# One order list for the third to the eleventh tile of a fused spectral filter and gated MLP; late row blocks by three rounded products

## The chip, the cores and the metric

One Trainium2 chip, one core, one launch. The metric is device microseconds (us). All times come from the runs, or from one profiled execution of the program.

## The reference

```python
def _A_ref(x, w_r, w_i):
    X = jnp.fft.rfft2(x, axes=(-2, -1))
    X = X * (w_r + 1j * w_i)
    return jnp.fft.irfft2(X, s=(S, D), axes=(-2, -1))

def _B_ref(x, w_gate, w_up, w_down):
    g = jnp.einsum("bsd,df->bsf", x, w_gate)
    u = jnp.einsum("bsd,df->bsf", x, w_up)
    return jnp.einsum("bsf,fd->bsd", _gelu(g) * u, w_down)

h = x + _A_ref(_layernorm(x), A_w_r, A_w_i)
out = h + _B_ref(_layernorm(h), B_w_gate, B_w_up, B_w_down)
```

x is 1 x 2048 x 512 in float32, the filter 2048 x 257, the hidden width of the MLP 1376. The norms have no weights and an eps of 1e-5.

## The kernel before

The 2048 rows are 16 row blocks of 128; a row of a block stays on a partition. The tensor `gh` holds all of them, first x, then the filter's output, then the sum.

*The filter.* The transforms are products with constant matrices, in full float32. START orders the norm and the transform over rows, SECOND the transform over columns, the filter and the first half of the way back. What is left is, for each block, a product over columns with `dis` (`over_d_back`, name U), an unfolding of even and odd parts (names V, X, K) and a product over rows with `mis` (M for blocks 0 to 7, "late" for blocks 8 to 15), then the residual with x and the statistics of the second norm (`stats2`).

*The MLP.* The hidden width is 11 tiles of 128 (`NF`), the rows are two halves of 1024. A tile's gate and up products for half of the rows are seven sums P0 to P6 (a Winograd form: 7 products for 8), each of two pairs. A float32 number is split into a rounded high part in the type fp32r and a low part, so a pair is three rounded products (`mm3`, high x high, high x low, low x high). The left factors are `cb` (the normalized rows, `combine`), the right ones `gu` (`load_gu`): two DMAs into `raw`, four steps on POOL that form differences, then the high part in one cast on DVE (or on ScalarE, with `by=act`) and the low part in three steps on POOL, for P0, for P1 to P3 and for P4 to P6. `raw` is one buffer; `gu` is two. ScalarE copies c1, c2 and c3 and DVE sums d1, dy, d2 let TensorE go on in the same banks (P2 needs c1, P4 needs c2, P5 needs c3, P6 needs dy). G, m, i and o are the gelu, the product with the up side, the rounding and the low part. `load_d` loads and splits a tile's rows of the down matrix (`wdr`, `wd`; name w). The down products add groups of two or three tiles into `gh`, block by block, through the banks 6 and 7 (`down`).

Tiles 0 to 10 serve the first half of the rows, 11 to 21 the second half, whose norm is put in late.

*What sets the order.* START, SECOND and FIRST are lists of names: within `tc.manual_schedule` each named engine works in the list's order, and waits only for data. FIRST covers the rest of the filter for blocks 0 to 7, the tiles 0 and 1 in two halves of the rows, and the first product of tile 2 (`g2P0`). In it r0 to r3 are the four steps on the weights of tile 2, hc the cast, lo1 to lo3 the low parts.

Tiles 2 to 10 are not in a list. A loop over n calls a generator for each tile (`gate_up` through `step`), one for the down products (`down` through `fill`) and one for each late block (`late`); only TensorE is held to the loop's order, and the other engines are put in order by the scheduler, with hints (`tc.issue_after`, `held`, `behind`). A late block's steps are: unfold (four POOL instructions on 128x256), load x, one float32 product with `mis`, residual, statistics. The second half follows the table SECOND_HALF, in a manual schedule of its own.

SP issues nearly all DMAs, in its program's order; it is in no list.

Of the kernel before, what the change touches and what calls it, by code (L numbers as in the profile page):

```python
# [49 lines left out]
u0.1 u4.0 w4 C4.0 V4.2 X4 w0 C0.1 V0.3 X0 U1.2 C1.4 V1.0 X1 r0 U5.3 C5.5 V5.1 M4.1 O4.0 M0.2 O0.1 U2.3 H4 H0 X5 C2.5  # L50
V2.3 M5.1 H5 I4 G4 O5.0 G0 I0 S4 S0 A4 A0 E0.5 U7.2 C7.1 M1.3 O1.1 g0awh H1 Q0 N0 U6.0 C6.0 V7.4 X2 U3.4 C3.5 I5 G5 S5
M2.1 V6.3 R00 I1 G1 S1 A5 A1 R01 U9.7 C9 H2 X7 V3.1 X3 T00 a0 Q1 T01.2 s0.0 O2.1 U8.4 C8 E1.6 N1 R11 M7.0 c0 d0 f0
U12.3 e0.1 k0 R10 H7 b0 O7.0 g0 h0 C12 X6 M6.4 H6 i0 j0 T11.1 s1.2 r1 l0 T10 c1 d1 G2 I2 M3.2 O3.1 H3 G7 a1 b1 I7 S7
O6.0 U15.3 C15 e1.0 f1 g1 U14.5 C14 U10.4 C10 m0 k1 n1 g0aP0 g0ac1 g1aP0 l1 g0aP3 g0aP1 G3 I3 S3 A7 A3 Q3 g0aP2 I6 n0
G6 h1 g1ac1 E3.7 N3 g1aP2 i1 R31 T31.5 g1aP1 o1 R30 T30 S2 S6 A6 A2 g1ac2 j1 E2.6 Q2 N2 o0 g1aP4 g0awl s3.6 c3 g0ac2
g0aP4 R20 T20 a3 g1ac3 g1aP5 d3 e3.4 K9.5 m1 g0ad1 g0ac3 g0aP5 f3 b3 h3 g0ady g0aP6 i3 j3 R21 T21.7 g3 g1aP3 a2 b2
g0bP0 g0bP1 g1bP0 K12.4 g1ad1 g1ady g1aP6 r2 l3 k3 s2.8 g1aG0 c2 d2 f2 e2.7 k2 g1bP1 g1am0 g0bc1 g2 g0bP2 g1bc1 r3 n3
n2 o3 g1bP2 g0ad2 o2 g0aG0 g0am0 l2 m2 m3 g0bP3 h2 K8.4 g0aG1 g0am1 g0bc2 g0bP4 g1bd1 i2 j2 g1bc2 g1bP4 g1bG0 g1ad2
g0bc3 g0bd1 g0bdy g0ai0 g0ao0 g1aG1 g1bP3 g1ai0 g1am1 g1bc3 g1bdy g0ai1 g0ao1 g0bP6 g0bd2 g1awh g1awl g1ai1 g0bG1
g0bP5 hc g1bP6 lo1 lo2 g0bG0 g0bm0 g0bi0 g1bP5 g1bm0 g1bi0 g1bd2 g1bG1 g0bo0 U13.7 C13 lo3 g0bm1 g0bi1 U11.6 C11 g1bm1  # L60
g1bi1 g1ao0 g0bo1 g1bo0 g1bo1 g1ao1 g2P0
# [5 lines left out]
b7 b8 p15 f14 b9 h f15 b10 h b11 b12 b13 b14 b15 h  # L67
"""
# [51 lines left out]
def kernel(  # L120
# [595 lines left out]
    def gate_up(n):  # L716

        do = products(n)[1] if n == 2 else tile_of(n)

        def all_of(names):  # L720
            for k in names.split():
                ins = do[k]()
            return ins

        all_of("P0")
        if n == 2:

            yield
            do = tile_of(n)
            all_of("c1 P1 d1")  # L730
        else:
            all_of("c1")
            yield
            all_of("P1 d1")
        yield
        for names in ("P2 c2", "P3"):
            all_of(names)
            yield
        last = copied[n] = all_of("P4 c3")
        all_of("dy")  # L740
        yield

        for _ in load_d(tiles[n][1], last):
            pass

        for names in ("P5", "P6 d2"):
            all_of(names)
            k = names[1] == "6"
            with tc.issue_after(last.ins):
                do[f"G{k:d}"]()  # L750
            all_of(f"m{k:d} i{k:d} o{k:d}")
            yield

    def down(group, last):


        banks = {}

        def add(i, fs, c=slice(0, D)):

            b = i
            r = slice(i % 4 * P, (i % 4 + 1) * P)
            if fs[0] == group[0]:
                banks[i] = next(bank_67)
            o = ps[:, banks[i], : c.stop - c.start]
            for f in fs:
                for ha, hw in ((0, 0), (0, 1), (1, 0)):
                    start, stop = f == group[0] and ha + hw == 0, f == group[-1] and ha == 1
                    pe.matmul(o, parts_of[tiles.index((0, f))][:, ha, i // 4, r], wds[f][:, hw, c], start=start, stop=stop)  # L769
            if fs[-1] == group[-1]:  # L770
                if last:
                    dve.scalar_tensor_tensor(gh[:, b, c], o, mv[:, b, 0:1], gh[:, b, c], op0=ALU.add, op1=ALU.add)
                    nc.sync.dma_start(o3[:, b, c], gh[:, b, c])
                else:
                    dve.tensor_tensor(gh[:, b, c], o, gh[:, b, c], op=ALU.add)  # L775

        if last:

            for fs in (group[:-1], group[-1:]):
                for i in range(2):  # L780
                    add(i, fs)
                    yield
        for i in range(2 if last else 0, 7):
            add(i, group)
            yield

        add(7, group)
        yield

    tiles = [(q, f) for q, order in enumerate(orders) for f in order]  # L790
    downs = iter(())
    begun_tiles, wds, parts_of, hns, copied, sums = {}, {}, {}, {}, {}, {}
    bank_67 = itertools.cycle((6, 7))
# [155 lines left out]
    def step(n):  # L949

        if n not in begun_tiles:
            f = tiles[n][1]
            if f not in gu:
                for _ in load_gu(f):
                    pass
            begun_tiles[n] = gate_up(n)
        next(begun_tiles[n])

    do["g2P0"] = lambda: step(2)
    et = mybir.EngineType  # L960
    with tc.manual_schedule(engines={et.PE, et.Activation, et.DVE, et.Pool}):
        for op in FIRST.split():
            name, *place = op.split(".")
            do[name](*map(int, place))


    def late(b):

        if b not in BY_THEN:

            with held("lo"):
                unfolded(b, row())
        yield
        xt = row()
        behind(nc.sync.dma_start(xt, x3[:, b]), pooled["raw"])
        py = ps[:, next(bank_67)]
        pe.matmul(py, mis[:, b], gh[:, b], start=True, stop=True)  # L977
        dve.scalar_tensor_tensor(gh[:, b], xt, mv[:, b, 0:1], py, op0=ALU.subtract, op1=ALU.add)  # L978
        for _ in stats2(b):
            pass  # L980
        yield

    def normed(b):

        hn = row()
        act.activation(hn, gh[:, b], AF.Copy, scale=rs2[:, b : b + 1])
        return hn

    def fill(n):
        for _ in range(n):  # L990
            next(downs, None)


    def second_half():
# [160 lines left out]
        yield  # L1155
# [86 lines left out]

    lates = {2: (9, 13), 3: (10,), 4: (14,), 5: (11,), 6: (15,)}
    ending = [late(b) for b in BY_THEN[:2]]
    for g in ending:
        next(g)
    downs = down(orders[0][:2], False)
    with tc.manual_schedule(engines={et.PE}):
        for n in range(2, NF):
            at_change = n == NF - 1  # L1250
            step(n)
            if n > 8:
                for i in range(2 * n - 18, 2 * n - 16):
                    with tc.issue_after(copied[n - 1].ins):
                        hns[i] = [normed(b) for b in (8 + i, 12 + i)]
            step(n)
            if at_change:
                second = second_half()
                with held("lo"):
                    next(second)  # L1260

                steps = [in_turn(i, hns[i], banks) for i, banks in enumerate(((3, 4), (5, 0), (3, 4), (1, 2)))]
                next(steps[0])
            for g in ending:
                next(g)
            if n in (6, 7):

                norm_scales(2 * n - 4, 2)
            if n == 7:
                sd = w3.tile([P, NB // 2], F32, name="sd", bufs=1)  # L1270
                dve.scalar_tensor_tensor(sd, mv2[:, NB // 2 :, 1], EPS, rs2[:, NB // 2 :], op0=ALU.add, op1=ALU.mult)
                kept_rows = [dram.tile([NB // 2, P], F32, name=f"rows{i}") for i in range(2)]
                for to, a in zip(kept_rows, (sd, mv[:, NB // 2 :, 0])):
                    nc.sync.dma_start(to.rearrange("b n -> n b"), a)
            fill(2)
            step(n)
            fill(2)
            step(n)
            fill(2)
            if at_change:  # L1280
                downs = down(orders[0][-3:], True)
                next(steps[0])
                next(steps[1])
            else:
                step(n + 1)
                fill(2)
            ending = [late(b) for b in lates.get(n, ())]
            for g in ending:
                next(g)
            step(n)  # L1290
            step(n)
            if n in (4, 7):
                downs = down(orders[0][: n + 1][-3:], False)
            if at_change:
                for s in steps:
                    for _ in s:
                        pass
                    fill(2)
                fill(12)
# [130 lines left out]
```

## Time and profile before

| | |
|---|---|
| median of three runs | 440.59 us (440.49 to 440.83) |
| the profiled execution | 440.44 us |
| its span | 438.6 us |
| PE busy | 432.1 us, 99% |
| POOL, DVE, ACT busy | 314.5, 313.3 and 243.0 us |
| DMA | 41.60 MB, mean 95 GB/s |
| granted clock of TensorE | full in every slice |

The span runs from the first to the last instruction of the profile; the 1.8 us between it and the execution's time lie around it. PE is TensorE's matmuls, PEld its weight loads, DVE VectorE, ACT ScalarE, POOL GpSimd, SP the queue that issues DMAs. A row of the timeline is start, duration, engine, line, operation, names of output and inputs, and how many; in brackets stands the idle time ahead of it on its engine, and what ended that. A float32 product of TensorE shows as two instructions. In time, START and SECOND fill the first 74 us, FIRST goes to about 121, tiles 2 to 10 to about 280, the second half to the end.

### The profile page before, as it was taken

How to read it: one execution, taken by the hardware profiler on the slowest of the kernel's cores; microseconds unless marked ns; L12 is line 12 of the kernel's file. 1: busy time of each engine (PE TensorE's matmuls, PEld its weight loads, DVE VectorE, ACT ScalarE, POOL GpSimd, SP SyncE). 2: the span in 40 equal slices, each digit the busy share in tenths (PEclk: the TensorE clock that was granted, in tenths of full speed). 3: DMA queues.
4: the chain of work that ended last, by engine and by line, in shares of the span. 5: the costliest groups of instructions: out<-in, count | busy, mean ns of one | idle time of the engine just before them, and what ended most of it. 6: DMA issues, size and time to landing. Idle time of an engine off the chain costs nothing.

```text
span 438.6 us, 6625 instructions
## 1 busy us (share of the span) xinstructions
PE 432.1 (99%) x2275; PEld 366.6 (84%) x2275; DVE 313.3 (71%) x577; ACT 243.0 (55%) x502; POOL 314.5 (72%) x346
## 2 busy tenths in 40 slices
PE   8999999999999999999999999999999999999996
PEld 8998999789978777877888888888888888888885
DVE  5968976897864766368734579578677786687785
ACT  5989785799712442124432787376455653565640
POOL 6987896999859788648644944067879779787821
PEclk9999999999999999999999999999999999999999
DMA  8996904320022112112220203501212021200005
GB/s 290 386 414 105 360 27 143 129 73 24 25 96 97 49 55 89 48 50 72 72 73 24 72 25 120 169 11 62 73 48 72 26 71 49 72 24 2 0 2 192
DMA packets 23542, 41.60 MB, mean 95 GB/s; under 512 B 4178, under 2 KB 9810, under 8 KB 23380
## 3 DMA queue, kind: packets, MB, share of 16 engines
q1 hardware_dynamic: 23220, 40.92, 28.0%
q8 instruction: 18, 0.29, 0.3%
q10 hardware_dynamic: 288, 0.26, 0.2%
q14 instruction: 16, 0.13, 0.1%
HBM read 36.97 MB, written 4.20 MB: 94 GB/s over the span
## 4 chain that ended last, share of the span: by engine, by line
PE 90%; POOL 4%; DVE 1%; issue 1%; DMA 1%; ACT 0%; SPq 0%; DVEq 0%; POOLq 0%
PE ps L163 16%; PE ps L165 16%; PE ps L164 16%; PE ps L769 14%; PE ps L1108 11%; PE ps L425 4%; PE ps L437 3%; PE ps L464 3%; PE ps L530 3%; POOL pn L339 2%; POOL pn L338 2%; PE ps L869 2%; PE ps L977 1%; DMA gh<-in_x 1%; PE ps L1214 1%
## 5 line engine op out<-in xcount | busy, mean ns | idle before, releaser
L163 PE MATMUL ps<-cb,gu 128*128 128x512 f32 (+1 forms) x336 | 127.2, 379 | 0.3 <-DVE a L695 0.3
L165 PE MATMUL ps<-cb,gu 128*128 128x512 f32 (+1 forms) x336 | 124.9, 372 | 0.0
L164 PE MATMUL ps<-cb,gu 128*128 128x512 f32 (+1 forms) x336 | 124.8, 372 | 0.0
L673 ACT ACTIVATE s<-ps 128x512 f32<-128x512 f32 (+1 forms) x72 | 40.5, 562 | 87.1 <-PE ps L165 86.7
L228 POOL TENSOR_TENSOR gu<-raw,gu 128x768 fp32r<-128x768 f32 (+1 forms) x42 | 61.3, 1481 | 29.1 <-DVE gu L223 16.8
L163 PEld LDWEIGHTS ps<-cb,gu 128*128 128x128 f32 x336 | 63.3, 188 | 12.2 <-issue 1.0
L164 PEld LDWEIGHTS ps<-cb,gu 128*128 128x128 f32 x336 | 63.3, 188 | 11.8 <-issue 1.0
L165 PEld LDWEIGHTS ps<-cb,gu 128*128 128x128 f32 x336 | 63.3, 188 | 11.1
L769 PE MATMUL ps<-wd,a 128*128 128x512 f32 x264 | 63.6, 393 | 0.0
L769 PEld LDWEIGHTS ps<-wd,a 128*128 128x128 f32 x264 | 49.1, 188 | 11.6 <-DVE gh L978 1.0
L682 DVE TENSOR_TENSOR ps<-ps,s 128x512 f32<-128x512 f32 (+1 forms) x48 | 31.1, 651 | 28.1 <-PE ps L165 25.3
L1115 DVE TENSOR_TENSOR gh<-ps,gh 128x512 f32<-128x512 f32 x66 | 44.3, 682 | 0.8 <-PE ps L1108 0.8
L679 ACT ACTIVATE s<-s 128x512 f32<-128x512 f32 (+1 forms) x48 | 28.4, 594 | 20.8 <-DVE s L676 20.7
L775 DVE TENSOR_TENSOR gh<-ps,gh 128x512 f32<-128x512 f32 x24 | 16.6, 691 | 25.8 <-PE ps L769 25.8
L676 DVE TENSOR_TENSOR s<-ps,s 128x512 f32<-128x512 f32 (+1 forms) x48 | 30.7, 641 | 5.8 <-PE ps L165 4.7
L511 POOL TENSOR_TENSOR wd<-wdr,wd 128x512 fp32r<-128x512 f32 x12 | 15.6, 1298 | 17.1 <-ACT wd L509 17.1
L676 DVE TENSOR_TENSOR ps<-ps,s 128x512 f32<-128x512 f32 (+1 forms) x24 | 15.7, 654 | 16.1 <-ACT s L673 15.6
L688 ACT ACTIVATE a<-ps 128x512 fp32r<-128x512 f32 (+1 forms) x26 | 13.8, 533 | 17.1 <-DVE ps L682 17.1
L207 POOL TENSOR_TENSOR raw<-raw 128x256 f32<-128x256 f32 x16 | 11.9, 741 | 15.6 <-DMA raw<-in_wgu 13.9
L1021 POOL TENSOR_TENSOR t<-mis,t 128x768 fp32r<-128x768 f32 (+1 forms) x9 | 13.3, 1479 | 13.3 <-ACT t L1019 13.2
L429 ACT ACTIVATE dp<-ps 64x512 f32<-64x512 f32 x32 | 19.0, 593 | 4.0 <-PE ps L425 3.6
L453 POOL TENSOR_TENSOR z<-t,t 128x520 f32<-128x520 f32 x15 | 19.5, 1298 | 2.1 <-DVE t L445 2.1
(183 smaller groups left out, 896.7 us busy)
## 6 DMA issues: line engine op xcount, KB each, us to landing
wt<-in_w SPq DMA_DIRECT2D x16, 520.0 KB, 7.2
raw<-in_wgu SPq DMA_DIRECT2D x32, 256.0 KB, 3.0
out<-gh SPq DMA_DIRECT2D x15, 256.0 KB, 2.0
gh<-in_x SPq DMA_DIRECT2D x7, 512.0 KB, 8.8
row<-in_x SPq DMA_DIRECT2D x12, 256.0 KB, 2.8
wdr<-in_wd SPq DMA_DIRECT2D x12, 256.0 KB, 2.6
mis<-in_wd SPq DMA_DIRECT2D x10, 256.0 KB, 2.7
a<-in_wgu SPq DMA_DIRECT2D x8, 256.0 KB, 3.1
```

What stands on the lines that cost most here:

```text
L163: pe.matmul(o, lh, rh, start=(i == 0 and not onto), stop=False, skip_group_check=True)
L164: pe.matmul(o, lh, rl, start=False, stop=False, skip_group_check=True)
L165: last = pe.matmul(o, ll, rh, start=False, stop=(i == n - 1), skip_group_check=True)
L228: pooled["lo"] = pool.tensor_tensor(r[:, 1, m], t[:, m], r[:, 0, m].bitcast(F32), op=ALU.subtract)
L453: eng.tensor_tensor(z[:, :, first], t1[:, :, first], t2[:, :, first], op=ALU.add)
L673: return lambda: act.activation(to, a, AF.Copy)
L676: return lambda: dve.tensor_tensor(to, a, b, op=ALU.add)
L679: return lambda: act.activation(g, g, AF.Gelu_apprx_tanh)
L682: return lambda: dve.tensor_tensor(u, u, g, op=ALU.mult)
L769: pe.matmul(o, parts_of[tiles.index((0, f))][:, ha, i // 4, r], wds[f][:, hw, c], start=start, stop=stop)
L1108: pe.matmul(ps[:, k], w[:, hw], a[ha], start=start and hw + ha == 0, stop=hw == 1, skip_group_check=True)
L1115: by.tensor_tensor(to, o, to, op=ALU.add)
```

## The change

Three things.

1. The loop over tiles 2 to 10 is replaced by a list, FIRST_HALF, in which all four engines have their order: `t5P0` is a product of tile 5, `y5.0` to `y5.8` are the nine steps of `load_gu` (0 the DMAs, 1 to 4 on raw, 5 the cast, 6 to 8 the low parts), `w` those of `load_d`, K, L, u, v, Y, R and B a late block's unfold, load, high part, low part, products, residual and statistics, D and E a down sum and its addition to `gh` (with a group and a block; F is the last tile's part of a sum), H, N and i the norm and the combination of the second half's rows, S0 the step that keeps the norm's factors as rows in DRAM (a DMA of 128 x 8 single numbers, read back later as rows, `dis<-rows`), Z the first loads of the second half. After @ stands the bank. The hints are gone but for those in `load_gu`.

2. A late block's float32 product is three rounded ones. `mis` of the late blocks is split once (mh on ScalarE, ml on POOL), the block itself by u on ScalarE and v on DVE.

3. Tile 2's weights are rounded by ScalarE in the three parts lo1 to lo3, and hc is gone. FIRST is written in another order and now holds P1 of tile 2 as well.

```diff
 FIRST = """
-u0.1 u4.0 w4 C4.0 V4.2 X4 w0 C0.1 V0.3 X0 U1.2 C1.4 V1.0 X1 r0 U5.3 C5.5 V5.1 M4.1 O4.0 M0.2 O0.1 U2.3 H4 H0 X5 C2.5
+u4.0 w4 u0.1 r0 C4.0 w0 C0.1 U1.2 C1.4 U5.3 C5.5 V4.2 X4 V0.3 X0 M4.1 O4.0 V1.0 M0.2 O0.1 X1 V5.1 X5 H4 G4 H0 I4 U2.3
...
+FIRST_HALF = """
+mh t2P2 t2P3 u8 v8 u12 v12 t2c2 L8 L12 y3.0 ml Y8@6 R8 B8.0 y3.1 y3.2 w2.0 u9 y3.3 y3.4 y3.5 y3.6 v9 t2G0 t2P4 Y12@7
...
+t10o1 i2l i1l Z4 i3T1 i3s i1c i1d i1f i1e i2c i1k i1n i2m i2d i2a i0n i3T0 E31 i3c i2e i2k i2n S0 i3l i1h D32@6 i3d
...
-    raw2 = load_gu(2)
+    raw2 = load_gu(2, by=act)
...
-    for k in ("r0", "r1", "r2", "r3", "hc", "lo1", "lo2", "lo3"):
+    for k in ("r0", "r1", "r2", "r3", "lo1", "lo2", "lo3"):
...
-        behind(nc.sync.dma_start(xt, x3[:, b]), pooled["raw"])
-        py = ps[:, next(bank_67)]
-        pe.matmul(py, mis[:, b], gh[:, b], start=True, stop=True)
...
+        def back_s(k):
+            nonlocal py
+            py = ps[:, k]
+            for hm, hu in ((0, 0), (1, 0), (0, 1)):
+                pe.matmul(py, mi2[:, hm, b - NB // 2], parts[hu], start=hm + hu == 0, stop=hu == 1)
...
+        def part(h):
+            parts[h] = rp.tile([P, D], F32R, name="row")
+            if h:
+                dve.tensor_tensor(parts[1], gh[:, b], parts[0].bitcast(F32), op=ALU.subtract)
             else:
+                act.activation(parts[0], gh[:, b], AF.Copy)
...
+        mi2 = w3.tile([P, 2, NB // 2, P], F32R, name="t", bufs=1)
+        act.activation(mi2[:, 0], mis[:, NB // 2 :], AF.Copy)
+
+    later["mh"] = high_of_mi
+    later["ml"] = lambda: pool.tensor_tensor(mi2[:, 1], mis[:, NB // 2 :], mi2[:, 0].bitcast(F32), op=ALU.subtract)
...
+        for op in FIRST_HALF.split():
+            name, _, place = op.partition("@")
+            later[name](*([int(place)] if place else []))
```

The tables START, SECOND and SECOND_HALF are the same.

More of the change, by code (lines that the diff above doesn't have):

```diff
@@ L714, in tile_of @@
         }
[L716 to L788, printed above, removed]
     tiles = [(q, f) for q, order in enumerate(orders) for f in order]
-    downs = iter(())
-    begun_tiles, wds, parts_of, hns, copied, sums = {}, {}, {}, {}, {}, {}
-    bank_67 = itertools.cycle((6, 7))
+    wds, parts_of, sums = {}, {}, {}
     def sum_tiles():
@@ L943, with tile_two @@
             half(n, h)
-    raw2 = load_gu(2)
+    raw2 = load_gu(2, by=act)
     next(raw2)
-    for k in ("r0", "r1", "r2", "r3", "hc", "lo1", "lo2", "lo3"):
+    for k in ("r0", "r1", "r2", "r3", "lo1", "lo2", "lo3"):
         do[k] = lambda: next(raw2)
[L949 to L959, printed above, removed]
-    et = mybir.EngineType
[L961 to L974, printed above, removed]
-        behind(nc.sync.dma_start(xt, x3[:, b]), pooled["raw"])
-        py = ps[:, next(bank_67)]
[L977 to L991, printed above, removed]
+    def tile_two():
+        products(2)[1]["P0"]()
+        yield
+        for k in ("c1", "P1", "d1"):
+            rest(2)[k]()
+        yield
+    rest = functools.cache(tile_of)
+    two = tile_two()
+    do["g2P0"] = do["g2P1"] = lambda: next(two)
+    et = mybir.EngineType
     def second_half():
@@ L1154, in second_half @@
             next(prepared[0])
-        yield
+            yield
         last_a, halves = None, {}
@@ L1241, in second_half @@
         end(3, 1, 1, halves=2)
[L1243 to L1283, printed above, removed]
-            else:
[L1285 to L1299, printed above, removed]
@@ new lines, with steps_named, later_tile @@
+    later = {}
+    groups = [orders[0][:2], orders[0][2:5], orders[0][5:8], orders[0][-3:]]
+    sd = w3.tile([P, NB // 2], F32, name="sd", bufs=1)
+    kept_rows = [dram.tile([NB // 2, P], F32, name=f"rows{i}") for i in range(2)]
+    def steps_named(name, gen, n):
+        for i in range(n):
+            later[f"{name}{i}"] = lambda: next(gen)
+    def later_tile(n):
+        for k in (f"P{m}" for m in range(7)):
+            later[f"t{n}{k}"] = functools.partial(lambda k: products(n)[1][k](), k)
+        for k in "c1 d1 c2 c3 dy G0 m0 i0 o0 d2 G1 m1 i1 o1".split():
+            later[f"t{n}{k}"] = functools.partial(lambda k: rest(n)[k](), k)
+        steps_named(f"w{n}.", load_d(tiles[n][1]), 2)
+        if n > 2:
+            steps_named(f"y{n}.", load_gu(tiles[n][1]), 9)
@@ new lines, in down, with multiply, begin, add @@
+    def down(g, i):
+        group, last, o = groups[g], g == 3, None
+        rows_of = slice(i % 4 * P, (i % 4 + 1) * P)
+        def multiply(fs):
+            for f in fs:
+                a = parts_of[tiles.index((0, f))]
+                for ha, hw in ((0, 0), (0, 1), (1, 0)):
+                    start, stop = f == group[0] and ha + hw == 0, f == group[-1] and ha == 1
+                    pe.matmul(o, a[:, ha, i // 4, rows_of], wds[f][:, hw], start=start, stop=stop)
+        def begin(k):
+            nonlocal o
+            o = ps[:, k]
+            multiply(group[:-1] if last and i < 2 else group)
+        def add():
+            if last:
+                dve.scalar_tensor_tensor(gh[:, i], o, mv[:, i, 0:1], gh[:, i], op0=ALU.add, op1=ALU.add)
+                nc.sync.dma_start(o3[:, i], gh[:, i])
+            else:
+                dve.tensor_tensor(gh[:, i], o, gh[:, i], op=ALU.add)
+        later[f"D{g}{i}"], later[f"E{g}{i}"] = begin, add
+        if last and i < 2:
+            later[f"F{g}{i}"] = lambda: multiply(group[-1:])
@@ new lines @@
+    for i, banks in enumerate(((3, 4), (5, 0), (3, 4), (1, 2))):
+        turned(i, banks)
+    later["N0"], later["N1"] = (functools.partial(norm_scales, b, 2) for b in (8, 10))
+    later["S0"] = keep_rows
+    second = second_half()
+    steps_named("Z", second, 5)
+    with tc.manual_schedule(engines={et.PE, et.Activation, et.DVE, et.Pool}):
+        for op in FIRST.split():
+            name, *place = op.split(".")
+            do[name](*map(int, place))
+        for op in FIRST_HALF.split():
+            name, _, place = op.partition("@")
+            later[name](*([int(place)] if place else []))
```

86 lines of the change are left out of this document (75 added, 11 removed).

## Prediction

> **What bounds the kernel now.** I read the busy times by stretch first, then the chain that ended last, then TensorE's gaps in the timeline.
>
> The stretches (us, then busy us of PE, PEld, DVE, ACT, POOL, then clock, DMA share, GB/s):
>
> ```profile
> 74.00:122.00 48.00, 47.71 (x355) 43.14 (x356) 39.91 (x101) 39.49 (x96) 43.55 (x58) 1.00 0.23 72
> 122.00:176.00 54.00, 53.95 (x227) 41.99 (x226) 33.78 (x54) 14.14 (x25) 41.41 (x44) 1.00 0.24 79
> 176.00:230.00 54.00, 54.00 (x236) 43.99 (x235) 31.29 (x65) 17.01 (x30) 32.11 (x34) 1.00 0.21 64
> 230.00:285.00 55.00, 55.00 (x260) 45.70 (x259) 35.25 (x61) 30.45 (x64) 26.07 (x31) 1.00 0.24 82
> ```
>
> ```profile
> PE 90%; POOL 4%; DVE 1%; issue 1%; DMA 1%; ACT 0%; SPq 0%; DVEq 0%; POOLq 0%
> ```
>
> From 74 us on TensorE is the bound and has nearly no hole. POOL is next: 43.55 of 48 us before 122, 41.41 of 54 after. The first list keeps its length, the second half its order, so there are two questions: how much TensorE work goes, and where TensorE starts to wait.
>
> **What goes.** A late row block's product of today, and the two waits that I find after 74 us:
>
> ```profile
> 157.31 0.39 PE L165 MATMUL ps<-cb,gu 128*128 128x512 f32 x1
> 157.54 1.02 PE L977 MATMUL ps<-gh,mis 128*128 128x512 f32 x2
> 157.99 0.80 PE L163 MATMUL ps<-cb,gu 128*128 128x512 f32 x1
> 158.63 0.40 PE L164 MATMUL ps<-cb,gu 128*128 128x512 f32 x1
> 119.44 0.50 PE L163 MATMUL ps<-cb,gu 128*128 128x512 f32 x1 [0.27 <-DVE a L695]
> 123.69 1.88 PE L977 MATMUL ps<-gh,mis 128*128 128x512 f32 x4
> 125.61 0.73 PE L769 MATMUL ps<-wd,a 128*128 128x512 f32 x2
> ```
>
> L165 to L977 is 0.23 us, the step of a rounded product. From L977 to the second rounded product behind it (158.63) are 1.09; less one step the block costs 0.86. Three rounded products cost 0.68. Eight blocks: 8 x 0.18 = 1.44 us less.
>
> The 0.27 at 119.44 comes from the third tile's rounding on DVE, which goes to ScalarE. At 125.61 four instructions of 0.43 us should have ended at 125.4; the 0.2 us wait for the residual goes, since in the list other products stand there. Together 0.47. The most that the change can bring is 1.9 us.
>
> ScalarE gets three roundings of the third tile in the first list (some 2 us), and in the second one of 128x1024 (mh) and eight of a row block, which the nearest row prices:
>
> ```profile
> L673 ACT ACTIVATE s<-ps 128x512 f32<-128x512 f32 x60 | 35.8, 596 | 86.4 <-PE ps L165 86.3
> ```
>
> 8 x 0.6 and about 1.0 for mh come to an engine that is busy 14 of 54 us after 122: free, but for mh, below.
>
> **r0 goes ahead of X4.** POOL's queue at the start of the first list (raw is the third tile's weights, row the unfolds that the products with mis need). Before:
>
> ```order
> L157 TENSOR_TENSOR gu_97<-raw_584,gu_97 128x256
> L887 TENSOR_TENSOR row_899<-row_897 128x2x128
> L887 TENSOR_TENSOR row_900<-row_898 128x2x128
> L887 TENSOR_TENSOR row_897<-row_901 128x2x128
> L207 TENSOR_TENSOR raw_922<-raw_922 128x256
> L887 TENSOR_TENSOR row_898<-row_902 128x2x128
> ```
>
> POOL's queue at the same place after the change (L231 was L207, L835 was L887):
>
> ```order
> L181 TENSOR_TENSOR gu_97<-raw_584,gu_97 128x256
> L231 TENSOR_TENSOR raw_922<-raw_922 128x256
> L835 TENSOR_TENSOR row_899<-row_897 128x2x128
> L835 TENSOR_TENSOR row_900<-row_898 128x2x128
> L835 TENSOR_TENSOR row_897<-row_901 128x2x128
> L835 TENSOR_TENSOR row_898<-row_902 128x2x128
> ```
>
> The step on the weights, which waits for their DMA, moved ahead of all the unfolds. What the trace says of these, with the same load for the fourth tile:
>
> ```profile
> 72.90 0.33 SPq L200 DMA_DIRECT2D raw<-in_wgu  x1
> 73.28 0.43 SPq L201 DMA_DIRECT2D raw<-in_wgu  x1
> 73.82 1.82 SPq L803 DMA_DIRECT2D a<-in_x  x4
> 76.33 2.12 POOL L887 TENSOR_TENSOR row<-row 128x256 f32<-128x256 f32 x3 [3.46 <-ACT row L856]
> 78.41 0.73 POOL L207 TENSOR_TENSOR raw<-raw 128x256 f32<-128x256 f32 x1
> 77.69 1.88 PE L869 MATMUL ps<-row,mis 128*128 128x512 f32 x4
> 122.50 0.33 SPq L200 DMA_DIRECT2D raw<-in_wgu  x1
> 126.16 0.74 POOL L207 TENSOR_TENSOR raw<-raw 128x256 f32<-128x256 f32 x1 [3.69 <-DMA raw<-in_wgu]
> ```
>
> From issue to first use took 3.66 us at 122.50; from 72.90 that is 76.56. Here four loads of x are issued right behind it, so I take 77.0. r0 and X4, 0.7 each, end at 78.4, and M4, which starts at 77.69 today with nothing idle ahead of it, starts at 78.5: 0.8 us lost, all of it TensorE's. Bounds: 0.4 (76.56) and 1.5 (0.7 later).
>
> **POOL's way to tile 5.** In the late blocks a rounding u on ScalarE and a subtraction v on DVE take the place of nothing. DVE's queue at the top of the new list (the first two rows belong to the first list and tile two, row<-gh,row is v8 and v12):
>
> ```order
> L719 TENSOR_TENSOR a<-ps,a 128x256 x3
> L700 TENSOR_TENSOR s_1478<-ps,s_1478 128x512
> L1207 TENSOR_TENSOR row<-gh,row 128x512 x2
> L1197 SCALAR_TENSOR_TENSOR gh<-row,mv,ps 128x512
> L544 BN_STATS bn<-gh 128x6
> L247 CAST gu<-raw 128x1792
> ```
>
> The same place before:
>
> ```order
> L695 TENSOR_TENSOR a<-ps,a 128x256 x5
> L676 TENSOR_TENSOR s_1476<-ps,s_1476 128x512
> L978 SCALAR_TENSOR_TENSOR gh<-row,mv,ps 128x512
> L520 BN_STATS bn<-gh 128x6
> L978 SCALAR_TENSOR_TENSOR gh<-row,mv,ps 128x512
> ```
>
> Two subtractions moved in ahead of the residual. v reads two tensors in SBUF; the DVE steps around it read one and PSUM. The trace has two such pairs with POOL at work, and a cast:
>
> ```profile
> 13.87 1.28 POOL L339 TENSOR_TENSOR pn<-gh 128x512 f32<-128x512 f32 x1
> 14.05 1.65 DVE L349 TENSOR_TENSOR uv<-pn 128x512 f32<-128x512 f32 x1
> 15.11 1.73 POOL L338 TENSOR_TENSOR pn<-gh 128x512 f32<-128x512 f32 x1
> 115.80 1.31 POOL L511 TENSOR_TENSOR wd<-wdr,wd 128x512 fp32r<-128x512 f32 x1
> 115.92 2.14 DVE L223 CAST gu<-raw 128x1792 fp32r<-128x1792 f32 x1
> ```
>
> L349 ended (15.70) 0.55 after POOL's L339 did (15.15), and POOL's next took 1.73 for 1.28: DVE waits out POOL's instruction, then POOL waits out DVE's. So a v costs POOL about 0.45, and a cast between POOL instructions about 1.0 (117.11 to 118.06).
>
> The Trainium skill, SBUF — State Buffer, "Who interferes with whom", says that a DVE instruction with two SBUF inputs contends with a GpSimd one that reads SBUF, and that the later fully blocks. By that rule each v would hold POOL a whole 0.6, not 0.45, and the sum would be some 0.8 higher; these rows agree in kind.
>
> Now POOL's queue ahead of tile 5's weights. Before:
>
> ```order
> L207 TENSOR_TENSOR raw_1761<-raw_1761 128x256
> L511 TENSOR_TENSOR wd_1701<-wdr_1699,wd_1701 128x512
> L211 TENSOR_TENSOR raw_1761<-raw_1761 128x256
> L213 TENSOR_TENSOR raw_1761<-raw_1761 128x256
> L215 TENSOR_TENSOR raw_1761<-raw_1761 128x256
> L228 TENSOR_TENSOR gu_97<-raw_1761,gu_97 128x256
> ```
>
> After the change (gh<-row and row<-gh are the unfolds K14 and K11):
>
> ```order
> L778 TENSOR_TENSOR row_1748<-gh_58 128x2x128
> L779 TENSOR_TENSOR row_1748<-gh_58 128x2x128
> L780 TENSOR_TENSOR gh_58<-row_1748 128x256
> L781 TENSOR_TENSOR gh_58<-row_1748 128x256
> L231 TENSOR_TENSOR raw_1708<-raw_1708 128x256
> L235 TENSOR_TENSOR raw_1708<-raw_1708 128x256
> L237 TENSOR_TENSOR raw_1708<-raw_1708 128x256
> L239 TENSOR_TENSOR raw_1708<-raw_1708 128x256
> L778 TENSOR_TENSOR row_1793<-gh_58 128x2x128
> L779 TENSOR_TENSOR row_1793<-gh_58 128x2x128
> L780 TENSOR_TENSOR gh_58<-row_1793 128x256
> L781 TENSOR_TENSOR gh_58<-row_1793 128x256
> ```
>
> Two unfolds that stood behind tile 5's weights stand ahead of them. POOL's prices:
>
> ```profile
> 128.62 0.73 POOL L215 TENSOR_TENSOR raw<-raw 128x256 f32<-128x256 f32 x1
> 129.39 1.09 DVE L223 CAST gu<-raw 128x1792 fp32r<-128x1792 f32 x1 [1.05 <-POOL raw L215]
> 130.56 4.35 POOL L228 TENSOR_TENSOR gu<-raw,gu 128x256 fp32r<-128x256 f32 x3 [1.21 <-DVE gu L223]
> 149.02 0.76 POOL L830 TENSOR_TENSOR row<-gh 128x256 f32<-128x256 f32 x1
> ...
> 151.27 0.74 POOL L833 TENSOR_TENSOR gh<-row 128x256 f32<-128x256 f32 x1
> 158.75 4.36 POOL L228 TENSOR_TENSOR gu<-raw,gu 128x256 fp32r<-128x256 f32 x3 [1.77 <-DVE gu L223]
> ```
>
> A tile's four steps on raw take 3.2 (126.16 to 129.35), the cast's wait 1.2, the three on gu 4.35: 8.75 in all. An unfold takes 2.95, a wd step 1.25 (1.31 in L511's row, less overlap).
>
> Start: tile two's first product ends at about 119.2 + 0.8 + 1.4 = 121.4; behind it on ScalarE stand its copy c1 and mh, 0.6 and 1.0; so ml begins on POOL at 123.0. No row has 128x1024; 0.55 per 256 columns more (0.73 for 256, 1.31 for 512) makes 2.4. POOL is free for tile 3 at 125.4, with its load landed. Then, to the end of tile 5's second lower part: tile 3 8.75; K13 2.95; the rest of tile 4's load, 3.66 less K13, 0.7; tile 4 3.2 + 1.25 + 2.95 (K10) + 4.35; a wd step 1.25; K14 2.95; tile 5's four 3.2; K11 2.95; 0.7 + 1.85 of its three lower parts. That is 37.05. To this come two casts that meet K10 and K11, 2.0, and five of the six v ahead of there (one falls into tile 4's load), 5 x 0.45 = 2.25: 41.3, so 166.7.
>
> TensorE would be at tile 5's P3, which needs that part, after 180 rounded products of the list, 180 x 0.227 = 40.9 us. The list begins at 119.44 - 0.27 + 12 x 0.227 = 121.9 today, 122.7 with the 0.8, so P3 is due at 163.6. It waits 3.1 in all, some of it already ahead of tiles 3 and 4 (an earlier wait only eats a later one). Today these parts were due later: the three of tile 5 began at 158.75, with no TensorE gap. Behind tile 5 a tile costs POOL 8.75 + 1.25 = 10 us and TensorE 42 x 0.227 = 9.5 and a third of 72 down products, 5.4: POOL catches up.
>
> The loads of x for blocks 8 and 12 now leave SP behind those of tile 3 and of a wd, at about 122.8, land 2.8 later (its row is below), at 125.6, and are needed behind Y8 at 126.1: hidden, by 0.5.
>
> Sum against the profiled execution (440.44, its span 438.6 and 1.8 around it): 440.44 - 1.44 - 0.47 + 0.8 + 3.1 = 442.4. The median of the runs is 0.15 above it: 442.5.
>
> **Rivals.**
>
> *POOL stays ahead (faster).* If v and cast find POOL between instructions, the 4.25 go, POOL ends at 162.5, ahead of 163.6, and only M4's 0.8 is left: a median of 439.5, 439.1 with the lower bound of M4. For it: POOL has gaps at loads, and TensorE ran without a hole over a list that kept POOL busy 43.55 of 48 us. Against it: in this stretch POOL has no gap to give. It decides where POOL's extra is under 1.1 us. Chance 0.2. Half the extra lets POOL end at 164.6, a wait of 1.0: 440.5, and 439.7 to 441.5 around it: 0.2.
>
> *The rows' way through DRAM.* The step S0 now stands behind E31, at the list's end; its DMA and the one that reads it back:
>
> ```profile
> 212.74 0.38 SPq L1274 DMA_DIRECT2D rows<-sd  x1
> 223.37 0.33 SPq L1133 DMA_DIRECT2D dis<-rows  x1
> dis<-rows SPq DMA_DIRECT2D x2, 256.0 KB, 3.6
> row<-in_x SPq DMA_DIRECT2D x12, 256.0 KB, 2.8
> a<-in_x SPq DMA_DIRECT2D x4, 256.0 KB, 4.8
> ```
>
> 10.6 us to land, then 3.6, then the copy to PSUM and, behind it on ScalarE, tile 11's c2, 0.6 each: 15.4. From S0 to tile 11's P4, which needs c2, TensorE has about 46 + 24 rounded products, 15.9 us. It is hidden by 0.5; loads and stores beside it (four loads of x took 4.8 where others take 2.8) would make it 1 to 2 us on top: 443.5 to 444.5. Behind the read on SP stand five stores and the load for tile 14, which is three tiles away: no one else waits. Chance 0.1.
>
> The Trainium skill, DMA: Bandwidth & Descriptors, "Anatomy of one DMA", gives about 2.0 us as the fixed cost. By it this small transfer lands 8.6 us sooner and the rival falls away; the row says otherwise.
>
> *The three products cost what the one did.* Then 1.44 come back, 443.9; the steps of rounded products speak against it: 0.02.
>
> **How the numbers follow.** The forecast (POOL late at tile 5) has 0.48, 441.4 to 443.6 by M4's bounds and one v or cast more or less. 0.2% is 0.9 us, about what a measurement of this kernel can tell from no change: faster is under 439.7, slower over 441.5. Faster: the rival's 0.2. Same: 0.2, the half case. Slower: the rest, 0.6. The range leaves out 0.1 below, in the faster rival, and 0.1 above: 439.2 to 443.9.
>
> **What would show it.** After the change: POOL's first step on raw ahead of the unfolds, M4 at 78.3 to 79.0 with an idle time that ends with POOL; v rows of over 1 us, and POOL rows lengthened by 0.45; TensorE waiting for POOL's step on gu at tiles 3 to 5, some 3 us in all; late products at 0.23 each. I am wrong if M4 does not wait, if tile 5's weights are ready before 163.6, or if TensorE's waits lie behind tile 5 (at the end of the list for dis).

## The result and the profile after

The changed kernel takes 446.02 us (median of 4 runs, 445.96 to 446.03), the kernel before 440.63 beside it: the ratio is 1.0121, 95% interval 1.0109 to 1.0133. It is slower, as forecast, but by 5.4 us where 1.9 were forecast. The profiled execution took 446.03, its span is 444.0.

The stretches of the changed kernel, columns as in the prediction, and one more at the change of halves; the last row is that stretch in the kernel before:

```profile
74.00:122.00 48.00, 47.65 (x356) 42.94 (x356) 37.92 (x100) 41.01 (x101) 43.99 (x58) 1.00 0.18 57
122.00:176.00 54.00, 52.33 (x225) 41.46 (x224) 38.68 (x55) 19.37 (x34) 48.63 (x48) 1.00 0.28 92
176.00:230.00 54.00, 54.00 (x237) 44.08 (x236) 33.16 (x69) 17.32 (x30) 31.17 (x29) 1.00 0.16 51
230.00:285.00 55.00, 55.00 (x257) 45.00 (x256) 36.19 (x63) 28.58 (x60) 25.80 (x31) 1.00 0.24 72
285.00:300.00 15.00, 13.90 (x60) 10.81 (x59) 9.41 (x15) 9.92 (x17) 6.97 (x6) 1.00 0.24 85
285.00:300.00 15.00, 15.00 (x68) 12.39 (x67) 10.92 (x18) 9.78 (x17) 11.02 (x9) 1.00 0.17 53
```

POOL went from 41.41 to 48.63 of the 54 us of the second stretch, and TensorE lost 1.7 us there. A second hole of 1.1 us is at 285 to 300. In the fourth stretch TensorE is full, and yet only 257 of its instructions start in it where 260 did before: busy, but slower.

TensorE's waits, from the view of waits (us, times, longest), and the chain that ended last:

```profile
PE ps L187 <- DVE a L719: 1.4, 1, 1.4
PE ps L187 <- DVE s L700: 0.9, 1, 0.9
PE ps L187 <- ACT s L697: 0.4, 2, 0.2
PE ps L817 <- POOL row L835: 0.3, 1, 0.3
```

```profile
PE 78%; DMA 6%; ACT 4%; DVE 4%; POOL 4%; issue 2%; DVEq 0%; SPq 0%; POOLq 0%; ACTq 0%
```

The first is the wait of tile 4's P0 at 150.3. The second and part of the third are at 292.7 and 295.3, where the second half begins; the fourth is M4. DMA's share of the chain went from 1% to 6%. Measured from start to start against the usual step, the holes are 0.45 (M4), 0.32 (Y8), 0.37 (tile 3's P4), 1.58 (tile 4's P0), 1.05 and 0.37 (second half): 4.1 us.

The slower steps show in the timeline. 18 down products before, and the row behind them:

```profile
221.00 4.24 PE L769 MATMUL ps<-wd,a 128*128 128x512 f32 x18
225.08 0.39 PE L163 MATMUL ps<-cb,gu 128*128 128x512 f32 x1
```

and in the changed kernel:

```profile
220.91 4.36 PE L1223 MATMUL ps<-wd,a 128*128 128x512 f32 x18
225.11 0.39 PE L187 MATMUL ps<-cb,gu 128*128 128x512 f32 x1
```

4.08 us for 18 are 226.7 ns each; 4.20 are 233.3. Nothing waits there. The prediction has no term for this. Over all rounded products of 512 columns behind 122 us (1313 records before, 1329 after), the steps exceed 226.7 ns by 0.5 us in sum before and by 3.5 after. So longer steps take 3.0 us. Holes and steps, 4.1 and 3.0, less the gains of 1.4 and 0.5 that the prediction had, make 5.2 of the 5.4 us between the two spans.

### The profile page after: what moved, and what is told of

Its sections match the earlier page's. It is cut to its first block, busy times and chain, and to the rows that moved or that the text cites. A ratio compares the mean times of both kernels' runs of the same rounds, so it can differ in the third digit from the quotient of the medians.

```text
span 444.0 us, 6657 instructions
## 1 busy us (share of the span) xinstructions
PE 434.8 (98%) x2283; PEld 367.2 (83%) x2283; DVE 321.2 (72%) x584; ACT 249.4 (56%) x514; POOL 321.4 (72%) x347
## 4 chain that ended last, share of the span: by engine, by line
PE 78%; DMA 6%; ACT 4%; DVE 4%; POOL 4%; issue 2%; DVEq 0%; SPq 0%; POOLq 0%; ACTq 0%
PE ps L187 14%; PE ps L189 14%; PE ps L188 14%; PE ps L1025 11%; PE ps L1223 8%; PE ps L449 3%; PE ps L461 3%; PE ps L554 3%; PE ps L488 3%; DMA dis<-rows 3%; DMA rows<-sd 2%; PE ps L817 2%; PE ps L1131 1%; ACT ts L404 1%; POOL gu L252 1%
## 5 line engine op out<-in xcount | busy, mean ns | idle before, releaser
L252 POOL TENSOR_TENSOR gu<-raw,gu 128x768 fp32r<-128x768 f32 (+1 forms) x42 | 62.2, 1499 | 28.9 <-DVE gu L247 14.2
L187 PEld LDWEIGHTS ps<-cb,gu 128*128 128x128 f32 x336 | 63.3, 188 | 15.5 <-DVE a L719 1.8
```

Source lines behind the costliest of these rows:

```text
L187: pe.matmul(o, lh, rh, start=(i == 0 and not onto), stop=False, skip_group_check=True)
L252: pooled["lo"] = pool.tensor_tensor(r[:, 1, m], t[:, m], r[:, 0, m].bitcast(F32), op=ALU.subtract)
```

## Experiments

Times are medians; a gain or loss is the difference from the changed kernel's 446.02 unless another kernel is named. Ratios are against the kernel before, run beside each.

**The address of wd.** The diff also takes the tile sd (8 columns, 32 bytes of each partition) at the start of the second list and no longer in tile 7. It now lies ahead of wdr and wd, and wd moves from byte 215360 to byte 215392 of a partition. Two runs, one on each kernel:

```diff
# e1_sd_padded: the changed kernel
-    sd = w3.tile([P, NB // 2], F32, name="sd", bufs=1)
+    sd = w3.tile([P, 32], F32, name="sd", bufs=1)[:, : NB // 2]
# e4_before_sd_first: the kernel before
     od_tile = w3.tile([P, 2, 256], F32, name="t", bufs=1)
+    sd = w3.tile([P, NB // 2], F32, name="sd", bufs=1)
...
-                sd = w3.tile([P, NB // 2], F32, name="sd", bufs=1)
```

> The changed kernel with the tile sd given 32 columns instead of 8, so that it takes 128 bytes of each partition and not 32; nothing else differs. In the changed kernel sd is taken ahead of the tiles wdr and wd, and pushes wd from byte 215360 of a partition, a multiple of 64, to byte 215392, which is not. Theory A (address): a product of 512 columns that streams from wd steps at 233 to 234 ns instead of 227, since 2048 bytes then lie in 33 stretches of 64 bytes instead of 32 (227 x 33/32 = 234); 264 products x 6.6 ns = 1.75, and about 1.05 more where wd is the stationary side in the second half: the kernel gets 2.8 us faster, to 443.2, and every step there goes back to 227. Theory B (order or port traffic makes these steps long): nothing moves, 446.0.

> The kernel before with its tile sd (8 columns, 32 bytes) taken at the start of the pool w3, ahead of wd, and not behind it; nothing else differs: wd then lies at byte 215392 as in the changed kernel. Theory A (address): the steps of products with wd go from 227 to 233 or 234 ns; the kernel before gets 2.8 us slower, 443.4. Theory B: no change, 440.6.

Moving sd alone in the kernel before costs 3.0 us: 443.59 (1.0065, 1.005 to 1.008). So it is the address. Its trace has these 3.0 us in the steps: 1.5 in the down products, 0.4 in the second half's products with wd, and 1.1 in products of cb and gu, none of whose tiles has moved (0.2 of it right ahead of a product with wd). But 128 bytes instead of 32 mended nothing: 446.12 (1.0122, 1.0107 to 1.0138). The down products of the first and of the second kernel:

```profile
220.98 4.36 PE L1223 MATMUL ps<-wd,a 128*128 128x512 f32 x18
225.17 0.39 PE L187 MATMUL ps<-cb,gu 128*128 128x512 f32 x1
```

```profile
222.12 4.36 PE L769 MATMUL ps<-wd,a 128*128 128x512 f32 x18
226.32 0.39 PE L163 MATMUL ps<-cb,gu 128*128 128x512 f32 x1
```

232.8 ns with wd at byte 215488, 233.3 at 215392, 226.7 at 215360. My rule of 64 bytes is wrong: 215488 is a multiple of 64. What the tiles of the kernel before have in common is byte 64 of 256. The next run puts wd there again:

```diff
-    sd = w3.tile([P, NB // 2], F32, name="sd", bufs=1)
+    sd = w3.tile([P, 64], F32, name="sd", bufs=1)[:, : NB // 2]
```

> The changed kernel with sd given 64 columns, 256 bytes of each partition; nothing else differs. Moving wd by 32 bytes slowed the kernel before by 3 us, and 128 bytes in place of 32 did not help the changed kernel, so a boundary of 64 or 128 bytes is not the rule. In the kernel before all tiles from which TensorE reads (cb, gu, a, row, t, wd) begin at the same byte of 256 (byte 64); behind 32 bytes wd begins at byte 96, behind 128 bytes at byte 192. Theory A (the two operands of a product must begin at the same byte of 256, else the stream and the weight load get into each other's way): with 256 bytes wd begins at byte 64 again, every step with wd goes back to 227 ns, 2.8 to 3.0 us faster, 443.1. Theory B (wd's distance from something else counts, or it must begin at exactly its old address): the steps stay at 229 to 241 and the time at 446.0.

443.56 (1.0066, 1.0051 to 1.0081): 2.46 faster, and 18 down products take 4.08 us. All steps together are 3.1 us shorter than in the changed kernel's trace; its holes are 0.8 longer (0.87 at M4, 0.55 at tile 3's P4, 1.26 in the second half), so the address is worth about 3 us, as in the kernel before:

```profile
220.57 4.24 PE L1223 MATMUL ps<-wd,a 128*128 128x512 f32 x18
224.65 0.39 PE L187 MATMUL ps<-cb,gu 128*128 128x512 f32 x1
```

Is byte 64 special, or the distance to other tiles? The first of two runs on the kernel before moves all these tiles by 32 bytes, the second only those behind cb:

```diff
# e11_before_all_moved
-    eps = base.tile([P, 32], F32, name="eps")[:, :1]
+    eps = base.tile([P, 40], F32, name="eps")[:, :1]
# e14_before_gap
     cb = w3.tile([P, 2, 7, 2, 4, P], F32R, name="cb", bufs=1)
+    gap = w3.tile([P, 8], F32, name="gap", bufs=1)
```

> The kernel before with its small tile eps given 40 columns instead of 32: 32 bytes more ahead of dis, mis, gu, row, cb, a, t and wd alike, which all begin at byte 96 of 256 then instead of byte 64; nothing else differs. Theory A (what counts is that the two operands of a product begin at the same byte of 256): no change, 440.6, rounded products still at 227 ns. Theory B (a fixed place counts, such as byte 64 of 256 or a multiple of 64): all of its rounded products step 4 to 7 ns longer, over 1500 of them: 446 to 451.

> The kernel before with an unused tile of 32 bytes taken behind cb, ahead of everything else in the pool w3: a, t and wd then all begin at byte 96 of 256, cb, gu, row and mis stay at byte 64; nothing else differs. Theory A (what counts is the byte of 256 of the two tiles of a product against each other): the 264 down products (wd with a) stay at 227 ns, as do those of a with wd and a with t; only the 78 products of row with t and row with wd take 229 to 236; in all under 0.6 slower, 440.7 to 441.3. Theory B (wd, or the weights, against a fixed place or against tiles of other products): the down products take 233 ns as with wd alone moved, 443.6.

All moved: 440.58 (0.9999, 0.999 to 1.0008), no change, although wd lies at byte 215392 again, as in e4_before_sd_first. It is a relation between tiles, not a place. With a, t and wd moved away from cb, gu and row: 443.41 (1.0061, 1.0044 to 1.0077), and my reading of the partner is only half right. Down products behind one another:

```profile
221.77 4.28 PE L770 MATMUL ps<-wd,a 128*128 128x512 f32 x18
225.88 0.39 PE L163 MATMUL ps<-cb,gu 128*128 128x512 f32 x1
```

With their partner moved along, they take 228.3 ns and not 233.3, and row's products take 230 (from start to start), as expected. But a product of cb and gu ahead of one with a moved tile takes 235 ns where it took 227, and the other products of cb and gu, of which no tile has moved, take 1 to 4 ns longer in the second half (means of 140, 140 and 77: 226.2, 227.0 and 227.2 before, 229.8, 228.5 and 230.4 here). At such a border the next product's weights are loaded beside the running stream (in this trace such a product of cb and gu starts at 401.214 us, the load for row with wd at 401.217). What lengthens the unmoved products is open. The other engines' tiles s1 to s3 moved too, but in e4_before_sd_first, where they did not, the same three means are 1 to 3 ns longer as well (228.9, 227.4 and 228.3).

**The rows' way through DRAM.**

```diff
-... t7P6 N1 t8P3 y9.2 ...
+... t7P6 N1 S0 t8P3 y9.2 ...
...
-... i2k i2n S0 i3l i1h ...
+... i2k i2n i3l i1h ...
```

> The changed kernel with the step S0 (the variances' factors and their store to DRAM) behind N1, in tile 7, as early as the kernel before has it; nothing else differs. Theory A (rows' way through DRAM, a rival of the prediction): the idle times of TensorE at 292.7 and 295.3, 1.05 and 0.37 us, go: 1.4 faster, 444.6, with the copy of dis to PSUM at about 286 instead of 290. Theory B (the copy waits for something else by then, or the next release is as late): under 0.4 faster.

444.70 (1.0088, 1.0071 to 1.0105): 1.32 faster, and no hole is left at the second half's start. In the changed kernel the read back of the rows and the copy that waits for it (SP's queue, then ScalarE) stand so:

```profile
268.69 0.38 SPq L1245 DMA_DIRECT2D rows<-sd  x1
277.61 0.33 SPq L1050 DMA_DIRECT2D dis<-rows  x1
283.64 0.33 SPq L1050 DMA_DIRECT2D dis<-rows  x1
```

```profile
283.01 0.60 ACT L1051 ACTIVATE ps<-dis 128x512 f32<-128x512 f32 x1 [1.54 <-DMA dis<-rows]
289.96 0.60 ACT L1051 ACTIVATE ps<-dis 128x512 f32<-128x512 f32 x1 [1.69 <-DMA dis<-rows]
```

8.9 us from S0's store to the first read, then 5.4 and 6.3 to the copies, with six stores of results and two loads issued between S0's store and the second read. The two reads go into the same tile, one behind the other: the second is issued 0.02 to 0.03 us behind the end of the first copy (here 283.62) in all seven traces that have S0 at this place. Behind the first copy TensorE has no hole; tile 11's c2, which stands behind it on ScalarE, ends at 284.2, 15.5 us behind the store. The holes at 292.7 and 295.3 come behind the second copy, the longer one through VectorE's products with it.

**GpSimd and VectorE at tiles 3 to 5.** VectorE's queue ahead of TensorE's wait at 150.3, then GpSimd's:

```profile
139.06 0.68 DVE L1207 TENSOR_TENSOR row<-gh,row 128x512 fp32r<-128x512 f32 x1
...
148.52 2.34 DVE L1207 TENSOR_TENSOR row<-gh,row 128x512 fp32r<-128x512 f32 x1 [2.25 <-ACT row L1209]
150.78 0.68 DVE L706 TENSOR_TENSOR ps<-ps,s 128x512 f32<-128x512 f32 x1
151.39 1.44 DVE L719 TENSOR_TENSOR a<-ps,a 128x512 fp32r<-128x512 f32 x2
```

```profile
147.09 0.74 POOL L781 TENSOR_TENSOR gh<-row 128x256 f32<-128x256 f32 x1
147.78 4.75 POOL L252 TENSOR_TENSOR gu<-raw,gu 128x256 fp32r<-128x256 f32 x3
```

v10 waits until GpSimd has unfolded block 10 (147.8) and ScalarE has rounded it; then it runs beside GpSimd's lower parts and takes 2.34 us, where v13 has 0.68. m1 and o0 of tile 2, for which TensorE waits, stand behind it. So v10 is moved back, and in a second run K11 too:

```diff
# e3_v_later
-... K10 y4.6 y4.7 u10 v10 y4.8 ... t3dy E07 t4c1 ...
+... K10 y4.6 y4.7 y4.8 ... t3dy E07 u10 v10 t4c1 ...
# e8_k11_later: the same, and
-... y5.4 K11 R13 ... w4.1 u11 y5.8 y6.0 ... t3m1 v11 R10 ... t4o0 t5c2 ...
+... y5.4 R13 ... w4.1 y5.8 K11 y6.0 ... t3m1 R10 ... t4o0 u11 v11 t5c2 ...
```

> The changed kernel with u10 and v10, the two parts of block 10, behind tile 3's dy instead of ahead of tile 2's last steps; nothing else differs. Theory A (VectorE's queue: v10 waits for GpSimd's unfolding and then runs 2.34 us beside GpSimd's lower parts, with tile 2's m1 and o0 queued behind it, for which TensorE's t4P0 waits): the idle time of 1.58 us at 150.3 goes: 1.2 to 1.6 faster, 444.4 to 444.8. Theory B (GpSimd itself is late by then, as the prediction has it): the wait comes back at the next use of tile 4's lower parts, under 0.5 faster.

> The changed kernel with u10 and v10 behind tile 3's dy (as in the run on that alone, where the wait at t4P0 went and 1.6 us of waits for GpSimd's lower parts came at tile 5, 163.1 to 166.4) and besides with block 11's unfold K11 behind tile 5's last lower part and u11, v11 behind tile 4's o0; nothing else differs. Theory A (GpSimd's way to tile 5, the prediction's third term): K11's 2.95 us off that way remove the wait: 1.6 faster, 444.4. Theory B (the wait only moves on again, to tile 6, or to Y11 and R11): under 0.5 faster, with TensorE idle behind 170.

v10 alone: 445.89 (1.0117, 1.0102 to 1.0132), nothing gained. The hole at 150.3 is gone, and TensorE waits for GpSimd at tile 5's P3, where the prediction put the wait:

```profile
163.95 0.40 PE L188 MATMUL ps<-cb,gu 128*128 128x512 f32 x1
165.15 0.50 PE L189 MATMUL ps<-cb,gu 128*128 128x512 f32 x1 [0.81 <-POOL gu L252]
```

With K11 off GpSimd's way: 444.35 (1.0083, 1.0066 to 1.01), 1.67 faster. Both holes are gone, and tile 3's P4 no longer waits (0.37); one of 0.74 is new at 174.1, where an add of down products (E) stands behind v11 in VectorE's queue. The second half's holes are 0.5 shorter in this trace (0.50 and 0.39).

**r0.**

```diff
-u4.0 w4 u0.1 r0 C4.0 ... M0.2 O0.1 X1 V5.1 ...
+u4.0 w4 u0.1 C4.0 ... M0.2 O0.1 X1 r0 V5.1 ...
```

> The changed kernel with r0 (GpSimd's steps on tile 0's raw weights) behind X1 and not ahead of X4, where the kernel before has it; nothing else differs. Theory A (prediction's first wait): M4's extra 0.45 to 0.75 us at 77.7 goes: 0.5 faster, 445.5. Theory B (r0 then is late for tile 0, or X1's wait replaces X4's): no change or slower, 446.0 or more.

445.08 (1.01, 1.0085 to 1.0115): 0.94 faster, M4's wait is gone. That is 0.45 of it; in this trace tile 3's P4 doesn't wait either (0.37), and the second half's holes are 0.15 shorter.

**One product instead of three** (in the changed kernel):

```diff
-            for hm, hu in ((0, 0), (1, 0), (0, 1)):
-                pe.matmul(py, mi2[:, hm, b - NB // 2], parts[hu], ...)
+            pe.matmul(py, mis[:, b], gh[:, b], start=True, stop=True)
...
+    later["mh"] = later["ml"] = lambda: None        # and u, v alike
```

> The changed kernel with the late row blocks by one unrounded product each, as the kernel before has them: no rounded parts (u, v), no parts of mi (mh, ml), Y with one product; the order of all else is the same. Prediction's prices: the eight Y cost 8 x 0.18 = 1.44 more. Theory A (the parts' work on GpSimd, ScalarE and VectorE causes the waits at Y8 and t4P0): 0.32 and 1.58 us of TensorE's idle time go, in sum 0.4 to 0.5 faster, about 445.5: the three products bring nothing here. Theory B (the waits come from the order of the unfolds): 1.44 slower, 447.4, with the waits still there.

443.29 (1.0063, 1.0048 to 1.0078): 2.73 faster, more than theory A's 0.5. The holes at Y8, tile 3's P4, tile 4's P0 and at the second half's start are all gone, 3.7 us against the 1.44 that the products save. The last of them (1.4) went although S0 stands where it stood: in this trace the second copy comes 4.7 us behind its read, not 6.3, and waits for nothing. Why that read came sooner is open.

**All together.** The edits of e5, e2, e7 and e8, and two moves more: u11, v11 behind E12, and Y8, R8, B8.0 behind tile 2's P4; then the same with one product.

> The changed kernel with everything that the runs so far point to: sd of 256 bytes (2.46 faster alone), S0 behind N1 (1.32), r0 behind X1 (0.94), u10, v10 and K11 later (1.67); and two small moves for the waits still seen there: u11, v11 behind E12 (TensorE's 0.74 at 174.1 behind v11's wait on VectorE), Y8 with R8 and B8.0 behind tile 2's P4 (0.32 at 125.5). Theory A (each is a wait or a step of its own on TensorE's path, so they add up): 446.0 - 6.4 - 0.7 = 438.9, between 438.5 and 439.7, faster than the kernel before by 0.2 to 0.5%. Theory B (they hide one another, one wait moving on to the next place): 440.5 or more.

> The kernel of the run before this one with the late row blocks by one unrounded product each (no u, v, mh, ml). In the changed kernel itself one product was 2.7 faster. Theory A (the three products do save 8 x 0.18 = 1.44 of TensorE's time, and what they cost there were the waits of their parts, which are gone here): 1.4 slower than the run before, 440.3. Theory B (the parts cost TensorE something other than those waits): as fast or faster, 438.9 or less.

444.34 (1.008, 1.0068 to 1.0093) and 441.06 (1.0009, 1.0 to 1.0018), because of my move of Y8. It put R8 behind v9 in VectorE's queue, and the down product that needs R8's bank waited. The wait of the first run, and its stretches (PE, clock, DMA share, GB/s among the columns):

```profile
PE ps L1223 <- DVE gh L1197: 3.6, 1, 3.6
```

```profile
127.00:131.00 4.00, 0.42 (x2) 0.00 (x0) 2.35 (x3) 0.32 (x1) 2.64 (x5) 0.85 0.00 0
131.00:136.00 5.00, 4.95 (x12) 3.88 (x13) 3.23 (x6) 0.00 (x0) 4.92 (x5) 0.50 0.07 23
136.00:141.00 5.00, 5.00 (x22) 4.11 (x21) 0.87 (x2) 0.00 (x0) 3.98 (x6) 0.93 0.23 82
```

A hole of 3.8 us, and then over 5 us at half the clock: 12 products where 22 fit. With Y8 back in its place:

> The kernel with all the moves together (sd of 256 bytes, S0 behind N1, r0 behind X1, u10, v10, K11, u11 and v11 later), with Y8, R8 and B8.0 back where the changed kernel has them. In the run with Y8 moved too, R8 stood behind v9 in VectorE's queue, TensorE idled 3.8 us at 127.0 for it and then ran at a granted clock of 0.5 from 131 to 136; those two cost 3.3 and 2.3 us of its 444.3. Theory A (the causes found account for all of the change's loss and add up): 444.3 - 5.6 = 438.7, between 438.3 and 439.3: 0.4% faster than the kernel before. Theory B (some of them only moved on, and the long wait hid it): 440.5 or more.

> The kernel of the run before this one with the late row blocks by one unrounded product each (no u, v, mh, ml). With Y8 moved, one product was 441.06 with a wait of 1.45 us at 127.3. Theory A (without waits for their parts the three products save 8 x 0.18 us): 439.6 to 440.1, that is 1.1 to 1.4 slower than the run before. Theory B (the three products' parts cost as much as they save in any order): as fast as the run before.

439.25 (0.9969, 0.9958 to 0.9981) with three products, 439.73 (0.9978, 0.9968 to 0.9987) with one. Both are faster than the kernel before, the first by 0.31%. Its stretch from 122 us on and TensorE's waits behind 74 us:

```profile
122.00:176.00 54.00, 53.94 (x236) 43.72 (x235) 37.73 (x55) 18.09 (x33) 48.06 (x49) 1.00 0.28 94
```

```profile
PE ps L1223 <- DVE gh L1235: 0.3, 1, 0.3
```

236 instructions where the changed kernel has 225. The gains of the single runs, 2.46 + 1.32 + 0.94 + 1.67, make 6.4, and 7.1 with 0.7 for the hole at 174.1; undone together they gave 6.77. This sum is looser than it looks: tile 3's P4 and a part of the second half's holes are in more than one of these gains (1.0 us twice), while 0.8 us of longer holes are missing from the first. The traces count each place once: against the changed kernel the holes fall from 4.1 to 0.75 us and the steps by 3.2, and the spans differ by 7.0. The three products are ahead by 0.48 and not by 1.44: 0.32 are still lost at Y8 and 0.43 at 180.2, both in waits that the kernel with one product doesn't have.

## Why the prediction was right or wrong

The sign was right. So were the gains, r0's wait and GpSimd's lateness, though that reached TensorE by a path the prediction didn't have. The size was not: the sum put two terms at nothing, the address of wd (3.0 us of longer steps) and the second of two reads of rows (1.4 us).

**The gains (1.44 and 0.47).** Right per product: a late block's three products take 0.68 us in the kernel with all the edits, as priced against 0.86 for the single one:

```profile
146.89 0.84 PE L1194 MATMUL ps<-row,t 128*128 128x512 f32 x3
147.57 0.39 PE L187 MATMUL ps<-cb,gu 128*128 128x512 f32 x1
```

Of the other gain, the wait of 0.27 is gone: nothing waits for the third tile's rounding at 119.55 now. What the parts cost elsewhere was priced as free ScalarE time, 2.4 us of GpSimd and 0.45 for each v; without them 2.3 us of holes go at Y8 and tiles 3 and 4.

**r0 ahead of X4 (0.8).** M4 was forecast at 78.3 to 79.0 behind a wait for GpSimd. It came at 78.25 with 0.45 of a hole, near the lower bound of the term; in the six other traces with r0 there the hole is 0.36 to 0.87. Undoing it took the hole away (e7). M4 in the changed kernel:

```profile
78.25 1.98 PE L817 MATMUL ps<-row,mis 128*128 128x512 f32 x4 [0.28 <-POOL row L835]
```

**GpSimd's way to tile 5 (3.1).** GpSimd was to end tile 5's second lower part at 166.7. It did at 166.8, and not by luck: ahead of there eight steps on GpSimd take longer than in the kernel before, by 4.1 us in all, where the sum had 4.25.

```profile
164.25 2.54 POOL L252 TENSOR_TENSOR gu<-raw,gu 128x256 fp32r<-128x256 f32 x2
```

TensorE lost 2.3 us by then (Y8, tile 3's P4, tile 4's P0), not 3.1, and not at GpSimd's parts: most of the wait, 1.58, reached it through VectorE, in whose queue v10 stood ahead of tile 2's m1. The prediction priced what a v takes from GpSimd; a v also holds up its own engine, 1.2 us in the mean of eight (three of them 1.2 to 2.5, five 0.7 to 0.8), with 2.3 of waiting ahead of v10:

```profile
L1207 DVE TENSOR_TENSOR row<-gh,row 128x512 fp32r<-128x512 f32 x8 | 9.5, 1200 | 2.3 <-ACT row L1209 2.3
```

I left out who stands behind v on its own engine. That the wait only changed its place is shown by e3, where 1.6 us of it come at tile 5; that GpSimd's length is its cause, by e8.

**The rows' way through DRAM.** Given 0.1 as a rival instead of the forecast, it came beside it, at 1.42 us. That this lies in the priced 1 to 2 is luck. The chain that was summed held: 15.4 us from S0 to the end of tile 11's c2 were forecast, 15.5 came (8.9 and 5.4 for 10.6 and 3.6), and TensorE didn't wait there. The step that failed is "no one else waits": a second read stands behind the first copy, 6.0 us behind the first read, and takes 6.3 more. With S0 early the first read is long done by then, and both holes are gone (e2). The 0.5 of cover was for the first read alone.

**What was missing.** sd's 32 bytes ahead of wd: 3.0 us of longer steps, of which 2.46 came back in e5, nearly half of the loss. The full diff shows the line; I read it as a change of time, not of place. Without it and the DRAM wait the changed kernel would stand near 442.2 by difference (446.02 - 2.46 - 1.32; no run has these two edits alone). That this is by the forecast's 442.5 is in part luck, since M4 and GpSimd's way cost 2.7 and not 3.9 in the profiled execution. None of the rivals of the other sign came: GpSimd did not stay ahead.

## What to carry to other kernels

Where an order is rewritten, ask of each new instruction that waits for a slow engine what stands behind it on its own engine. A wait that is removed at one place comes back at the next user unless the work behind it gets shorter, so undo one edit and look where the hole goes. Ask of a transfer that is read back whether one buffer takes several reads, and follow the chain to the last of them. Treat a moved allocation as a change of the kernel: keep tiles from which TensorE reads at the same byte of 256 (of offsets, 32, 128 and 256 bytes were tried here), and compare the start-to-start step of the same products in both traces before looking for waits.

## What was not expected of the hardware

The step of a product depends on where tiles lie against each other: 226.7 ns with all at the same byte of 256, 233.3 (down products) with wd 32 bytes off, 232.8 at 128 off. The Trainium skill, SBUF — State Buffer, "Who interferes with whom", gives TensorE independent ports for the moving operand and for the weights and says "PE and ACT never wait on anyone"; these runs show TensorE slowed by an address alone, so not both can hold for them. Which of the two fails, its own two reads meeting or another engine's, no run shows.

A hole of 3.8 us halved the granted clock: the 13 products from 131.06 us on took 5.67 us where 13 usual steps are 2.95, so it cost 2.7 us more. A hole of 1.58 us left the clock at 1.00. The Trainium skill, TensorE: Matmul & The Clock Gate, "Part 1: The HAM clock gate", puts the fall to half rate behind an idle window of about 3.4 us. The lengths of both holes agree with it, the moment does not quite: a clock of 0.85 over 127 to 131 us is 1.2 us at half, so it fell near 129.8, 2.4 us behind the end of the last product (127.42).
